# Half of an attention's split products from float32r to float16, from the second batch on

## The chip, the core and the metric

The kernel runs on one core of a Trainium2 chip. The metric is the device time of one execution in microseconds (us); lower is better. The names of the engines are those of the profile: PE (TensorE matmul), PEld (its weight loads), DVE (VectorE), ACT (ScalarE), POOL (GpSimd), SP (SyncE, which issues all DMAs here).

## What is computed

A linear attention with exponential features feeds a feed-forward layer (called MoE in the code; it has one expert). All inputs are float32.

```python
batch, n_heads, seq, head_dim = (8, 8, 576, 64); d_feat = 128
def phi(x):
    proj = np.einsum('bhsd,df->bhsf', x, w_phi)
    proj = proj - np.max(np.abs(proj), axis=-1, keepdims=True)
    return np.concatenate([np.exp(proj), np.exp(-proj)], axis=-1)
q_p, k_p = (phi(q), phi(k))
kv = np.einsum('bhsf,bhsd->bhfd', k_p, v)
z = np.sum(k_p, axis=2)
num = np.einsum('bhsf,bhfd->bhsd', q_p, kv)
den = np.einsum('bhsf,bhf->bhs', q_p, z)[..., None] + 1e-06
x = (num / den), heads side by side: 4608 rows x 512
h = x @ w_in                                  # 512 x 2048
out = (h * (1.0 / (1.0 + np.exp(-1.702 * h)))) @ w_out   # 2048 x 512
```

In the code t is the projection less its largest magnitude. exp(t) is at most 1; exp(-t) can be large.

## The kernel before

The program is first recorded and then put in order by a list scheduler (class Recorder): each operation has an estimated cost, a priority from a table of due times (`R.part(v0, v1)`; one unit is 384 rows through the MoE), and the buffers that it needs. The scheduler simulates the five engines with these costs and emits all instructions in the order that comes out. Every instruction so has the same source line, L346, and each engine works through its list strictly in that order.

**Attention.** A batch has four pairs of heads (hp 0 to 3); a pair is a unit, so there are 32 units, 0 to 31. Units 0 to 5 are "exact" (plain float32 products); the 26 units from 6 on are not, and of these the change speaks most. A unit covers 512 of the 576 positions; the other 64 of all heads are a batch's tail (`attn_tail`). In a unit that is not exact, every factor of a product is split into a high part and a low part, and three of the four partial products are summed in PSUM. For k and for q and for each head (four times a unit), `features_k` or `features_q` makes e = [exp(t), exp(-t)] (128 x 1024, two ACT instructions), and `parts` makes eh = e rounded to float32r (one ACT copy of 1024) and el = e - eh (one DVE subtraction of 1024). v is split in the same way into vs (one ACT copy, one DVE subtraction). The products kv <- vs,eh and vs,el then run: a hi matmul of 132 columns (the weights are eh, the moving operand both parts of v) and a lo matmul of 66 (weights el, moving the high part of v). The first half (s = 0) of e is exp(t), the second (s = 1) exp(-t). The sum kf is split into kzs (ACT copy, then a subtraction, on POOL from batch 1 on), and the numerators and denominators are the products kzs,eh (132) and kzs,el (66). The division makes xf, which is split into float16 halves xo and transposed by DMA into x[b], the MoE's input. The tail's products are vts,ekth/ektl and kzs,eqth/eqtl.

**MoE.** Each factor is split into two float16 parts with power-of-two scales. One step j (16 a chunk) has 12 matmuls hb <- x,wbuf a 384 rows, then ACT th (tanh), DVE g, ACT gh, DVE gl, and 9 matmuls ab <- wbuf,gh/gl of 512 columns. Attention of later batches is interleaved with the chunks. There are three x buffers; x[b] takes the place of x[b-3] (for batch 2: of `kept`, the half sums of the first 512 rows) when the MoE has read it.

**Scales.** `batch_max(sb, stage)` finds the largest magnitude of v for two batches: two DMAs of 1152 KB into the new x buffer, each followed by a DVE reduction of 2304 columns, and then `vg`, its power of two. Before, `csx` = vg * 2^-13 enters only at the division, in `inverse`, and the part has priority u + 0.975 (u is the batch's due time), so the first units of a batch do not wait for it.

Of the kernel before, what the change touches and what calls it, by code (L numbers as in the profile page):

```python
# [20 lines left out]
P = 128  # L21
D = 64
# [327 lines left out]
def attn_moe_kernel(ctx, tc, q, k, v, w_phi, w_in, w_out, out):  # L350
# [25 lines left out]
    def static(name, shape, dt):  # L376
# [13 lines left out]
        e=([P, 1024], F32), eh=([P, 1024], F32R), el=([P, 1024], F32R),  # L390
        ekth=([P, 1024], F32R), ektl=([P, 1024], F32R),
        eqth=([P, 1024], F32R), eqtl=([P, 1024], F32R),
# [9 lines left out]
    }  # L402

# [175 lines left out]
    csx = static("csx", [P, B // SB], F32)  # L579
# [70 lines left out]

    pools["zt"] = buf("zt", [P, 2, NHP, 2, D], F16, 1)
# [7 lines left out]
    nc.gpsimd.memset(f32(vs0), 0.0)  # L659
    nc.gpsimd.memset(f32(vs0[:, :, 0, D : D + 1]), 1.0)  # L660
    nc.gpsimd.memset(f32(vt0), 0.0)
# [3 lines left out]
    for a in range(2):  # L665
        r = slice(a * D, a * D + D)
        nc.gpsimd.memset(f32(vt0[r, :, a, 0, D : D + 1]), 1.0)
# [78 lines left out]
    def features_k(t, exact, hi="eh", lo="el"):  # L746

        e = new("e")
        e4 = e.rearrange("p (a s f) -> p a s f", a=4, s=2)
        R.scalar.activation(e4[:, :, 0], t, AF.Exp)  # L750
        R.scalar.activation(e4[:, :, 1], t, AF.Exp, scale=-1.0)
        return [x.rearrange("p (a f) -> p a f", a=4) for x in parts(e, exact, hi, lo)]

    def features_q(t, exact, hi="eh", lo="el"):
# [6 lines left out]
        R.scalar.activation(e2[:, 0], qt, AF.Exp)  # L761
        R.scalar.activation(e2[:, 1], qt, AF.Exp, scale=-1.0)
        return [x.rearrange("p (s n) -> p s n", s=2) for x in parts(e, exact, hi, lo)]

    def attn_tail(tl, exact, bank):
# [6 lines left out]
        ekt = features_k(tk, False, "ekth", "ektl")  # L772
        eqt = features_q(tq, False, "eqth", "eqtl")
        vt = new("vts")
        for a in range(2):
            r = slice(a * D, a * D + D)
            R.scalar.copy(vt[r, :, a, 0, 0:D], tl[r, 2])
            R.vector.tensor_sub(vt[r, :, a, 1, 0:D], tl[r, 2], f32(vt[r, :, a, 0, 0:D]))
        return ekt, eqt, vt
# [27 lines left out]
    def attn_unit(b, hp, nat, tail, nt, x32, x16, exact, bank):  # L807
# [5 lines left out]
        if exact:  # L813
            tk = project_whole(kq[:, 0], bank)
        else:
            scales = kq_scales(kq)
            tk = project(kq[:, 0], (scales[0], scales[0]), bank)
        if exact:
            vv = vn
        else:  # L820
            vv = new("vs")
            R.scalar.copy(vv[:, :, 0, 0:D], vn[:, :, 0:D])
            R.vector.tensor_sub(vv[:, :, 1, 0:D], vn[:, :, 0:D], f32(vv[:, :, 0, 0:D]))
        kf = new("kf")
        if exact:
            kvt = psa()[0:DV]
            for h in range(2):
                ek = features_k(tk[h], exact)[0]
                mm = [(vv[:, 4 * h + t], ek[:, t]) for t in range(4)]
                for i, k in ((0, 0), (0, 1), (1, 0)):  # L830
                    mm.append((vt[:, hp, h, k], ekt[i][:, hp]))
                products(True, True, [(x, y, kvt[:, 256 * h : 256 * h + 256]) for x, y in mm])
            across(kvt, kf.rearrange("p s h d -> p h s d"))
        for h in range(0 if exact else 2):
            ek = features_k(tk[h], exact)
            kv = psa()[:, 0 : 4 * DV].rearrange("p (s c) -> p s c", s=2)
            mm = []
            for t in range(5):
                for s in range(2):
                    f = slice(s * NF, (s + 1) * NF)  # L840
# [9 lines left out]
        R.scalar.copy(kz[:, :, :, 0], kf)  # L850
        (R.vector if b == 0 else R.gpsimd).tensor_sub(
            kz[:, :, :, 1], kf, f32(kz[:, :, :, 0])
        )
# [10 lines left out]
        def numden(slots, dst):  # L864
# [6 lines left out]
            for i, (h, j) in enumerate(slots):  # L871
                for s in range(2):
                    if j < 4:
                        st = [e[:, s, j * P : (j + 1) * P] for e in eqs[h]]
                        o, m = nd[:, i].unsqueeze(1), kz[:, s, h : h + 1]
                    else:
                        st = [e[:, s, hp * P : (hp + 1) * P] for e in eqt]
                        o, m = nd[:, i : i + 2], kz[:, s]
# [18 lines left out]
        def inverse(den, n):  # L897
# [3 lines left out]
                rc, den, EPS, csx[:, b // SB : b // SB + 1], ALU.add, ALU.mult  # L901
# [27 lines left out]
        if x32 is not None:  # L929
            j0 = TX // P  # L930
            tp = psa()
            for j in range(j0):
                R.tensor.transpose(tp[:, j * P : (j + 1) * P], xj[:, j], ident)
            R.scalar.activation(
                x32[:, hp], tp[:, 0:TX], AF.Copy, scale=csx[:, b // SB : b // SB + 1]
            )
# [160 lines left out]
    xs = {}  # L1097
    V1 = (-1.1375, 0.5)
# [9 lines left out]
    def attention(b):  # L1108
# [105 lines left out]
```

## Time and profile before

| | |
|---|---|
| median of 3 runs | 1141.74 us (1139.68 to 1143.14) |
| the profiled execution, its own time | 1139.36 us |
| its span in the trace | 1137.6 us |
| PE busy | 1098.4 us (97%), 8879 matmuls |
| DVE busy | 846.4 us (74%) |
| ACT busy | 706.1 us (62%) |
| POOL busy | 176.9 us (16%) |
| mean granted TensorE clock | 0.986 |

Busy is the time in which an engine had at least one instruction in work. Matmuls overlap in the pipeline, so a matmul's own duration is not what it costs PE; the distance from its start to the next one's is. The 1.8 us between span and time lie outside the trace.

### The profile page before, as it was taken

The page shows a single profiled execution, that of the slowest core. Times are in us where ns is not written, and L with a number is a line of the kernel's source. Part 1 is how long each engine was busy: PE and PEld are TensorE (multiplying, and loading weights), DVE is VectorE, ACT ScalarE, POOL GpSimd, SP SyncE. Part 2 cuts the span into 40 slices and gives each one's busy share as a digit, 9 for nine tenths or more (in the row PEclk, how much of TensorE's full clock was granted, in tenths as well). Part 3 has the DMA queues.
Part 4 walks back from the last instruction along what each step waited for, and adds up shares of the span by engine and source line. Part 5 has one row for each costly group of instructions (what it writes and reads, how often), then busy time and mean ns, then how long its engine had stood idle before and what let it go on. Part 6 is the DMA issues. An engine that isn't in the chain of part 4 may idle for free.

```text
span 1137.6 us, 22238 instructions
## 1 busy us (share of the span) xinstructions
PE 1098.4 (97%) x8879; PEld 842.6 (74%) x8879; DVE 846.4 (74%) x1642; ACT 706.1 (62%) x1333; POOL 176.9 (16%) x169
## 2 busy tenths in 40 slices
PE   5997999999999999999999999989999999999997
PEld 4664667878887778778888787778887788767653
DVE  5899978999779888786669988887577976523322
ACT  4676786874767766674667766665566776533323
POOL 6545000120111211020011211120111211110000
PEclk9997999999999999989999999989999999999999
DMA  8854214344223262332133243332232230010101
GB/s 270 282 162 148 43 38 95 78 100 124 60 63 80 56 159 57 80 84 48 27 77 79 67 109 96 70 84 48 33 80 57 48 66 11 10 38 1 28 1 28
DMA packets 172520, 87.76 MB, mean 77 GB/s; under 512 B 140032, under 2 KB 164736, under 8 KB 171392
## 3 DMA queue, kind: packets, MB, share of 16 engines
q1 hardware_dynamic: 172416, 86.34, 31.1%
q8 instruction: 69, 1.13, 0.4%
q14 instruction: 35, 0.29, 0.1%
HBM read 54.59 MB, written 9.44 MB: 56 GB/s over the span
## 4 chain that ended last, share of the span: by engine, by line
PE 87%; DVE 6%; ACT 2%; DMA 2%; issue 1%; POOL 1%; SPq 1%; ACTq 0%; DVEq 0%; POOLq 0%
PE ab L346 34%; PE hb L346 32%; PE at L346 21%; DVE el L346 1%; DVE sm L346 1%; DMA x<-in_v_dram 1%; DVE gl L346 1%; DVE sc L346 1%; SPq L346 1%; DVE wbuf L346 1%; DVE t L346 1%; DVE g L346 0%; DMA xT<-xs 0%; ACT e L346 0%; DVE ks L346 0%
## 5 line engine op out<-in xcount | busy, mean ns | idle before, releaser
L346 PE MATMUL hb<-x,wbuf 128*128 128x192 f16 (+3 forms) x3264 | 490.8, 285 | 1.9 <-DVE g L346 1.9
L346 PE MATMUL ab<-wbuf,gh 128*128 128x512 f16 x1152 | 348.2, 386 | 0.8 <-ACT gh L346 0.7
L346 PEld LDWEIGHTS <-wbuf 128*128 128x128 f16 x3264 | 286.3, 99 | 65.8 <-issue 2.8
L346 ACT ACTIVATE th<-hb,usc 128x384 f32<-128x384 f32 (+1 forms) x208 | 115.6, 556 | 143.1 <-PE hb L346 139.5
L346 PE MATMUL ab<-wbuf,gl 128*128 128x512 f16 x576 | 201.2, 386 | 0.5 <-DVE gl L346 0.3
L346 DVE SCALAR_TENSOR_TENSOR g<-th,hb 128x384 f32<-128x384 f32 (+1 forms) x208 | 107.6, 518 | 108.5 <-ACT th L346 106.2
L346 PEld LDWEIGHTS <-gh 128*128 128x128 f16 x1152 | 110.8, 98 | 79.8 <-ACT gh L346 2.4
L346 DVE TENSOR_TENSOR el<-e,eh 128x1024 fp32r<-128x1024 f32 x104 | 128.1, 1233 | 38.9 <-ACT eh L346 20.4
L346 PE MATMUL at<-kzs,eh 128*128 128x132 f32 x416 | 156.2, 378 | 0.1
L346 PE MATMUL at<-vs,eh 128*128 128x132 f32 x416 | 153.6, 372 | 2.6 <-ACT e L346 1.5
L346 PE MATMUL at<-vs,el 128*128 128x66 f32 x416 | 144.2, 347 | 1.2 <-DVE el L346 1.2
L346 PE MATMUL at<-kzs,el 128*128 128x66 f32 x416 | 144.9, 351 | 0.4 <-DVE el L346 0.4
L346 ACT ACTIVATE gh<-g,al 128x384 f16<-128x384 f32 (+1 forms) x176 | 106.5, 606 | 62.1 <-DVE g L346 61.9
L346 DVE SCALAR_TENSOR_TENSOR gl<-g,al,gh 128x384 f16<-128x384 f32 (+1 forms) x176 | 113.0, 642 | 43.1 <-ACT gh L346 36.8
L346 ACT CAST eh<-e 128x1024 fp32r<-128x1024 f32 x104 | 108.8, 1047 | 3.8 <-PE at L346 2.8
L346 DVE TENSOR_REDUCE sm<-at 128x4 f32<-128x512 f32 x126 | 86.1, 684 | 32.3 <-PE at L346 32.1
L346 POOL TENSOR_TENSOR xf<-nf,rc 128x512 f32<-128x512 f32 x28 | 31.1, 1111 | 454.0 <-DVE rc L346 374.6
L346 PE MATMUL at<-ph,xT 128*128 128x128 f16 x944 | 90.7, 221 | 0.0
L346 PEld LDWEIGHTS at<-vs,eh 128*128 128x128 f32 x416 | 84.4, 203 | 6.8 <-ACT e L346 1.7
L346 DVE SCALAR_TENSOR_TENSOR t<-at,ks,sm 128x512 f32<-128x512 f32 x118 | 87.9, 745 | 1.7
L346 PEld LDWEIGHTS at<-kzs,eh 128*128 128x128 f32 x416 | 84.2, 202 | 6.7 <-issue 2.9
L346 PEld LDWEIGHTS <-gl 128*128 128x128 f16 x576 | 56.3, 98 | 43.5 <-DVE gl L346 2.7
(157 smaller groups left out, 1722.5 us busy)
## 6 DMA issues: line engine op xcount, KB each, us to landing
x<-in_v_dram SPq DMA_DIRECT2D x8, 1152.0 KB, 6.1
vn<-in_v_dram SPq DMA_DIRECT2D x64, 128.0 KB, 2.8
kq<-in_k_dram SPq DMA_DIRECT2D x32, 256.0 KB, 3.0
kq<-in_q_dram SPq DMA_DIRECT2D x32, 256.0 KB, 2.9
x<-in_moe_w_in_dram SPq DMA_DIRECT2D x10, 512.0 KB, 5.1
x<-in_moe_w_out_dram SPq DMA_DIRECT2D x10, 512.0 KB, 5.5
out_dram<-osb SPq DMA_DIRECT2D x40, 128.0 KB, 2.4
out_dram<-osb SPq DMA_DIRECT2D x16, 256.0 KB, 2.4
```

Source lines behind the costliest of these rows:

```text
L346: f(*[g(a) for a in o.args], **{k: g(a) for k, a in o.kw.items()})
```

## The change

From batch 1 on, everything that belongs to exp(t) (s = 0) is held in float16: eh6, el6 and their like for the tail, the split of v (v6, vt6) and the split of kf (kz6). What belongs to exp(-t) (s = 1) stays float32r. Both sets of products add into the same PSUM tiles. For the range of float16, v is first multiplied by iv = 1/vg, a power of two; `csx` is then a constant except in batch 0, and its piece at the transposition (dead code here, TX = 0) goes. In detail:

- `parts` has no copy any more: ACT computes exp twice, once into e (float32) and once straight into the high part, each 512 wide; DVE subtracts 512 at a time. The float32r pools shrink to 512.
- `split_v`: ACT writes the float16 high part of v * iv, DVE the float32r low part, and POOL copies each into the other type.
- kz is split per s: two ACT copies and two POOL subtractions of 132 in place of one of 264.
- `batch_max` is put earlier in the due times (u - 0.1 in place of u + 0.975), and the v split of batches 2, 4 and 6 needs its result.
- Exact units: the tail's three products of 256 columns a head become six of 128.

```diff
-        e=([P, 1024], F32), eh=([P, 1024], F32R), el=([P, 1024], F32R),
+        e=([P, 1024], F32), eh=([P, 512], F32R), el=([P, 512], F32R),
...
+    for nm in ("eh", "el", "ekth", "ektl", "eqth", "eqtl"):
+        pools[nm + "6"] = buf(nm + "6", [P, 512], F16, NB[nm])
...
+        R.vector.reciprocal(iv[:, sb : sb + 1], vg[:, sb : sb + 1])
...
-    def parts(e, exact, hi, lo):
+    def two(nm, b, spare):
+
+        return new(nm + "6") if b else new(spare), new(nm)
+
+    def parts(b, src, e, hi, lo):
+
+        his, los = two(hi, b, "eh"), two(lo, b, "el")
+        for i, sg in enumerate((1.0, -1.0)):
+            R.scalar.activation(e[i], src, AF.Exp, scale=sg)
+            R.scalar.activation(his[i], src, AF.Exp, scale=sg)
+            h = his[i] if i == 0 and b else f32(his[i])
+            R.vector.tensor_sub(los[i], e[i], h)
+        return list(zip(his, los))
...
-        eh, el = new(hi), new(lo)
-        R.scalar.copy(eh, e)
-        R.vector.tensor_sub(el, e, f32(eh))
-        return eh, el
...
+    def split_v(dst, d16, src, sc):
+
+        R.scalar.activation(d16[0], src, AF.Copy, scale=sc)
+        R.vector.scalar_tensor_tensor(dst[1], src, sc, d16[0], ALU.mult, ALU.subtract)
+        R.gpsimd.tensor_copy(dst[0], d16[0])
+        R.gpsimd.tensor_copy(d16[1], f32(dst[1]))
...
-            R.scalar.copy(vv[:, :, 0, 0:D], vn[:, :, 0:D])
-            R.vector.tensor_sub(vv[:, :, 1, 0:D], vn[:, :, 0:D], f32(vv[:, :, 0, 0:D]))
+            vv = (new("v6"), new("vs"))
+            split_v(
...
-                    st = [e[:, t, f] for e in ek] if t < 4 else [e[:, hp, f] for e in ekt]
-                    vx = vv[:, 4 * h + t] if t < 4 else vt[:, hp, h]
+                    st = [e[:, t] for e in ek[s]] if t < 4 else [e[:, hp] for e in ekt[s]]
+                    vx = vv[s][:, 4 * h + t] if t < 4 else vt[s][:, hp, h]
...
+            kz = [new("kz6"), kz[:, 1]]
+            for s in range(2):
+                R.scalar.copy(kz[s][:, :, 0], kf[:, s])
+                R.gpsimd.tensor_sub(
+                    kz[s][:, :, 1], kf[:, s], f32(kz[s][:, :, 0]) if s else kz[s][:, :, 0]
+                )
...
-                R.part(u + 0.975, u + 0.975)
+                z = u - VB if b else u + 0.975
+                R.part(z, z)
```

The scheduler makes a new order of it. On PE, in the middle of the kernel, while the MoE reads the third x buffer (x_114), the rows before read as follows (hb and ab are the MoE; kzs and vs with eh or el are float32r products, whose weight load is part of the instruction; a float16 product has a row LDWEIGHTS of its own):

```order
L346 LDWEIGHTS wbuf_156
L346 MATMUL hb_65<-x_114,wbuf_156 128x384
L346 MATMUL at_62<-kzs_105,eh_97 128x132
L346 LDWEIGHTS wbuf_156
L346 MATMUL hb_65<-x_114,wbuf_156 128x384
L346 MATMUL at_62<-kzs_105,el_98 128x66
L346 LDWEIGHTS wbuf_156
L346 MATMUL hb_65<-x_114,wbuf_156 128x384
L346 MATMUL at_62<-kzs_105,eh_97 128x132
```

Now, at the like place (v and its eh, el here are the float16 ones):

```order
L346 MATMUL at_63<-vs_180,eh_97 128x132
L346 LDWEIGHTS gh_120
L346 MATMUL ab_67<-wbuf_165,gh_120 128x512
L346 MATMUL at_63<-vs_180,el_98 128x66
L346 LDWEIGHTS eh_141
L346 MATMUL at_63<-v_183,eh_141 128x132
L346 LDWEIGHTS gl_122
L346 MATMUL ab_67<-wbuf_165,gl_122 128x512
L346 MATMUL at_61<-kzs_105,eh_96 128x132
L346 LDWEIGHTS el_144
L346 MATMUL at_63<-v_183,el_144 128x66
```

A float32r product still has a MoE matmul ahead of it; every second attention product is now a float16 one, which may stand behind a float32r one.

On DVE, where batch 2 begins, the v split of unit 8 stood before ahead of both reductions of batch_max (sc <- x), at 0.92 units of MoE progress, with the maximum's power of two (vg) far behind, after unit 10's split. The rows there now (g and gl are the MoE's):

```order
L346 TENSOR_REDUCE sc_138<-sc_137 128x1
L346 SCALAR_TENSOR_TENSOR gl_121<-g_117,al_172,gh_119 128x256
L346 TENSOR_REDUCE sc_133<-at_62 1x1
L346 SCALAR_TENSOR_TENSOR gl_122<-g_118,al_172,gh_120 128x256
L346 TENSOR_SCALAR sc_133<-sc_133 1x1 x2
L346 COPY vg_179<-at_62 128x1
L346 TENSOR_SCALAR osc_177<-mg_173,vg_179 128x1
L346 TENSOR_SCALAR usc_176<-wg_169,vg_179 128x1 x2
L346 RECIPROCAL iv_175<-vg_179 128x1
L346 SCALAR_TENSOR_TENSOR vs_180<-vn_71,iv_175,v_183 128x8x64
L346 SCALAR_TENSOR_TENSOR vts_181<-tl_88,iv_175,vt_184 64x4x64 x2
```

The first v split of batch 2 stands right behind iv, at 1.67 units of MoE progress in place of 0.92; by unit 11 (2.19 in both) the two orders are level again, and from unit 17 on the new one is level or up to half a unit ahead (unit 25: 7.12 before, 6.94 now).

On POOL a unit in the middle of the kernel read kzs, xf, xo before; now:

```order
L346 CAST vs_180<-v_183 128x8x64
L346 CAST v_183<-vs_180 128x8x64
L346 TENSOR_TENSOR kz_182<-kf_106,kz_182 128x2x66
L346 TENSOR_TENSOR kzs_105<-kf_106,kzs_105 128x2x66
L346 TENSOR_TENSOR xf_104<-nf_109,rc_139 128x2x4x64
L346 TENSOR_TENSOR xo_111<-xf_104,xo_111 128x512
```

Two copies have come in ahead of the subtractions, and one subtraction has become two of half the size.

## Rows read from the trace of the kernel before

**Rows 1.** Windows by stretch: busy us (instructions) by engine, clock, DMA share, GB/s.

```profile
0.00:140.00 140.00, 116.39 (x677) 78.79 (x678) 118.81 (x226) 89.42 (x172) 65.40 (x59) 0.95 0.60 184
140.00:481.80 341.80, 340.85 (x2981) 270.26 (x2978) 293.11 (x591) 236.46 (x465) 40.99 (x40) 1.00 0.35 81
481.80:509.40 27.60, 25.11 (x220) 21.81 (x219) 22.69 (x55) 19.05 (x35) 7.18 (x7) 0.88 0.41 100
744.00:771.80 27.80, 24.62 (x218) 21.04 (x217) 23.61 (x52) 21.31 (x39) 7.08 (x6) 0.88 0.33 86
771.80:1000.30 228.50, 228.50 (x1931) 183.55 (x1929) 162.35 (x301) 143.64 (x269) 31.04 (x32) 1.00 0.22 44
```

**Rows 2.** Groups by form, PE: count, busy us, mean ns, idle before them.

```profile
L346 PE MATMUL at<-kzs,eh 128*128 128x132 f32 x416 | 156.2, 378 | 0.1
L346 PE MATMUL at<-vs,eh 128*128 128x132 f32 x416 | 153.6, 372 | 2.6 <-ACT e L346 1.5 <-ACT eh L346 0.7 <-ACT ls L346 0.3
...
L346 PE MATMUL at<-ph,xT 128*128 128x128 f16 x944 | 90.7, 221 | 0.0
...
L346 PE MATMUL at<-vts,ekth 128*128 128x132 f32 x104 | 39.3, 379 | 0.0
...
L346 PE MATMUL at<-kzs,eqth 128*128 128x264 f32 x52 | 22.0, 440 | 0.0
...
L346 PE MATMUL hb<-x,wbuf 128*128 128x64 f16 x192 | 10.7, 194 | 0.0
```

**Rows 3.** Timeline of PE, 369 to 371 us: start, duration, instruction, count.

```profile
368.97 1.46 PE L346 MATMUL hb<-x,wbuf 128*128 128x384 f16 x8
...
370.30 0.34 PE L346 MATMUL hb<-x,wbuf 128*128 128x384 f16 x1
370.34 0.36 PE L346 MATMUL at<-vs,eh 128*128 128x132 f32 x1
370.54 0.34 PE L346 MATMUL hb<-x,wbuf 128*128 128x384 f16 x1
370.58 0.33 PE L346 MATMUL at<-vs,el 128*128 128x66 f32 x1
370.75 0.34 PE L346 MATMUL hb<-x,wbuf 128*128 128x384 f16 x1
```

**Rows 4.** Timeline of PE: float16 matmuls of 128 and of 64 columns.

```profile
278.77 0.41 PE L346 MATMUL hb<-x,wbuf 128*128 128x64 f16 x8
...
366.05 0.61 PE L346 MATMUL at<-ph,xT 128*128 128x128 f16 x8
```

**Rows 5.** Groups by form, DVE and ACT: the split before and its nearest kin.

```profile
L346 DVE TENSOR_TENSOR el<-e,eh 128x1024 fp32r<-128x1024 f32 x104 | 128.1, 1233 | 38.9 <-ACT eh L346 20.4 <-PE at L346 18.2
...
L346 ACT CAST eh<-e 128x1024 fp32r<-128x1024 f32 x104 | 108.8, 1047 | 3.8 <-PE at L346 2.8
...
L346 ACT ACTIVATE e<-t 128x512 f32<-128x512 f32 x144 | 86.5, 629 | 2.2 <-DVE el L346 1.7 <-PE at L346 0.4
...
L346 DVE TENSOR_TENSOR vs<-vn,vs 128x512 fp32r<-128x512 f32 x26 | 17.9, 688 | 8.7 <-ACT vs L346 8.5
```

**Rows 6.** Groups by form, POOL: a subtraction and a copy.

```profile
L346 POOL TENSOR_TENSOR kzs<-kf,kzs 128x264 fp32r<-128x264 f32 x28 | 21.2, 756 | 278.4 <-ACT kzs L346 266.7 <-issue 11.7
...
L346 POOL COPY wb<-wst 64x128 f32<-64x128 f32 x2 | 0.6, 304 | 1.4 <-DMA wst<-in_w_phi_dram 1.3
```

**Rows 7.** Timeline of all engines, 889 to 892 us: POOL and DVE at the same time.

```profile
889.43 1.88 POOL L346 TENSOR_TENSOR xo<-xf,xo 128x512 f16<-128x512 f32 x1 [1.73 <-ACT xo L346]
890.21 1.52 DVE L346 SCALAR_TENSOR_TENSOR gl<-g,al,gh 128x384 f16<-128x384 f32 x1
```

**Rows 8.** Timelines of DVE and PE: unit 20's v split and its first product.

```profile
606.64 0.69 DVE L346 TENSOR_TENSOR vs<-vn,vs 128x512 fp32r<-128x512 f32 x1
...
624.84 0.33 PE L346 MATMUL at<-vs,eh 128*128 128x132 f32 x1
```

**Rows 9.** DMA issues, and the group of batch_max's reductions on DVE.

```profile
x<-in_v_dram SPq DMA_DIRECT2D x8, 1152.0 KB, 6.1
...
L346 DVE TENSOR_REDUCE sc<-x 128x1 f32<-128x2304 f32 x8 | 20.3, 2543 | 0.9 <-DMA x<-in_v_dram 0.9
```

More of the change, by code (lines that the diff above doesn't have):

```diff
@@ L649, in attn_moe_kernel @@
     pools["vts"] = buf("vts", [P, NHP, 2, 2, DV], F32R, 1)
+    pools["kz6"] = buf("kz6", [P, 2, 2, DV], F16, 1)
+    pools["v6"] = buf("v6", [P, 8, 2, DV], F16, 1)
+    pools["vt6"] = buf("vt6", [P, NHP, 2, 2, DV], F16, 1)
     pools["zt"] = buf("zt", [P, 2, NHP, 2, D], F16, 1)
@@ L658, in attn_moe_kernel @@
     vs0, vt0 = pools["vs"].aps[0], pools["vts"].aps[0]
-    nc.gpsimd.memset(f32(vs0), 0.0)
-    nc.gpsimd.memset(f32(vs0[:, :, 0, D : D + 1]), 1.0)
-    nc.gpsimd.memset(f32(vt0), 0.0)
+    v60, vt60 = pools["v6"].aps[0], pools["vt6"].aps[0]
+    for ap in (f32(vs0), v60, f32(vt0), vt60):
+        nc.gpsimd.memset(ap, 0.0)
+    for ap in (f32(vs0), v60):
+        nc.gpsimd.memset(ap[:, :, 0, D : D + 1], 1.0)
     nc.gpsimd.memset(pools["zt"].aps[0], 0.0)
@@ L666, in attn_moe_kernel @@
         r = slice(a * D, a * D + D)
-        nc.gpsimd.memset(f32(vt0[r, :, a, 0, D : D + 1]), 1.0)
+        for ap in (f32(vt0), vt60):
+            nc.gpsimd.memset(ap[r, :, a, 0, D : D + 1], 1.0)
     def kq_scales(kq):
@@ L771, in attn_tail @@
             tk, tq = project(n, kq_scales(tl[:, 0:2]), bank)
-        ekt = features_k(tk, False, "ekth", "ektl")
-        eqt = features_q(tq, False, "eqth", "eqtl")
+        ekt = features_k(b, tk, False, "ekth", "ektl")
+        eqt = features_q(b, tq, False, "eqth", "eqtl")
         vt = new("vts")
+        if b == 0:
+            for a in range(2):
+                r = slice(a * D, a * D + D)
+                R.scalar.copy(vt[r, :, a, 0, 0:D], tl[r, 2])
+                R.vector.tensor_sub(
+                    vt[r, :, a, 1, 0:D], tl[r, 2], f32(vt[r, :, a, 0, 0:D])
+                )
+            return ekt, eqt, (vt, vt)
+        vt6 = new("vt6")
         for a in range(2):
             r = slice(a * D, a * D + D)
-            R.scalar.copy(vt[r, :, a, 0, 0:D], tl[r, 2])
-            R.vector.tensor_sub(vt[r, :, a, 1, 0:D], tl[r, 2], f32(vt[r, :, a, 0, 0:D]))
-        return ekt, eqt, vt
+            split_v(
+                [vt[r, :, a, i, 0:D] for i in range(2)],
+                [vt6[r, :, a, i, 0:D] for i in range(2)],
+                tl[r, 2],
+                iv[r, b // SB : b // SB + 1],
+            )
+        return ekt, eqt, (vt6, vt)
     def products(first, last, mm):
@@ L817, in attn_unit @@
             tk = project(kq[:, 0], (scales[0], scales[0]), bank)
+        sc = iv[:, b // SB : b // SB + 1]
         if exact:
-            vv = vn
-        else:
-            vv = new("vs")
-            R.scalar.copy(vv[:, :, 0, 0:D], vn[:, :, 0:D])
-            R.vector.tensor_sub(vv[:, :, 1, 0:D], vn[:, :, 0:D], f32(vv[:, :, 0, 0:D]))
+            if b:
+                R.scalar.activation(vn[:, :, 0:D], vn[:, :, 0:D], AF.Copy, scale=sc)
+        else:
+            vv = (new("v6"), new("vs"))
+            split_v(
+                [vv[1][:, :, i, 0:D] for i in range(2)],
+                [vv[0][:, :, i, 0:D] for i in range(2)],
+                vn[:, :, 0:D],
+                sc,
+            )
         kf = new("kf")
@@ L827, in attn_unit @@
             for h in range(2):
[L828 to L832, printed above, removed]
+                ek = features_k(b, tk[h], True)
+                o = kvt[:, 256 * h : 256 * h + 256]
+                mm = [(vn[:, 4 * h + t], ek[:, t], o) for t in range(4)]
+                for s in range(2):
+                    for i, k in ((0, 0), (0, 1), (1, 0)):
+                        mm.append(
+                            (vt[s][:, hp, h, k], ekt[s][i][:, hp], o[:, s * NF : s * NF + NF])
+                        )
+                products(True, True, mm)
             across(kvt, kf.rearrange("p s h d -> p h s d"))
         for h in range(0 if exact else 2):
-            ek = features_k(tk[h], exact)
+            ek = features_k(b, tk[h], False)
             kv = psa()[:, 0 : 4 * DV].rearrange("p (s c) -> p s c", s=2)
@@ L849, in attn_unit @@
         kz = new("kzs")
[L850 to L853, printed above, removed]
+        if b == 0:
+            R.scalar.copy(kz[:, :, :, 0], kf)
+            R.vector.tensor_sub(kz[:, :, :, 1], kf, f32(kz[:, :, :, 0]))
+            kz = [kz[:, s] for s in range(2)]
+        else:
+            kz = [new("kz6"), kz[:, 1]]
+            for s in range(2):
+                R.scalar.copy(kz[s][:, :, 0], kf[:, s])
+                R.gpsimd.tensor_sub(
+                    kz[s][:, :, 1], kf[:, s], f32(kz[s][:, :, 0]) if s else kz[s][:, :, 0]
+                )
         if exact:
@@ L900, in inverse @@
             R.vector.tensor_scalar(
-                rc, den, EPS, csx[:, b // SB : b // SB + 1], ALU.add, ALU.mult
+                rc, den, EPS, csx if b == 0 else 2.0**-13, ALU.add, ALU.mult
             )
@@ L910, in attn_unit @@
                 products(
-                    True, True, [(kf[:, s, h], eqs[h][0][:, s], ndt) for s in range(2)]
+                    True, True, [(kf[:, s, h], eqs[h][:, s], ndt) for s in range(2)]
                 )
@@ L928, in attn_unit @@
         xj = xf.rearrange("p j a d -> p j (a d)")
[L929 to L936, printed above, removed]
         if exact:
```

54 lines of the change are left out of this document (29 added, 25 removed).

## The prediction

> **What bounds the kernel now.** I read the windows by stretch first [rows 1]. From 140 us on PE is the bound: it is busy for 340.85 of 341.80 us up to 481.8 us, and for all of 771.8 to 1000.3 us. DVE is the next engine, with 293.11 of 341.80 us (86%) in the first of these stretches and 71% in the second; ACT has 69% and 63%. Three places differ. In the first 140 us PE idles for 23.6 us while the weights arrive and DVE is busy for 118.81 us. At 481.8 to 509.4 us and at 744.0 to 771.8 us PE loses 2.5 and 3.2 us idle, and the granted clock is 0.88, so part of each stretch ran at 1.2 GHz in place of 2.4: some 3.3 us more in each (0.12 of 27.7). There the MoE has used up the x that it has, and attention is what PE waits for. Everything else is PE's own work, so a saving on PE counts nearly whole, if the others keep up.
>
> Then the groups of PE [rows 2] give the counts, and the timelines [rows 3, 4] what a matmul really costs. The reader is to look at starts, not durations. Eight MoE matmuls of 384 columns take 1.46 us with the last one's 0.34 in it: 0.16 us each. From 370.30 to 370.75 there are two of these and one float32r pair (132 and 66 columns): 0.45 - 0.32 = 0.13 us for the pair, though each of them shows over 0.33 us. Eight float16 matmuls of 128 columns take 0.61 us with a last one of 0.22 [rows 2, 4], so 56 ns each; of 64 columns (0.41 - 0.19) / 7 = 31 ns, each with a weight load of its own.
>
> **The change, step by step.** The sum is made against the profiled execution's 1139.4 us, which is 2.4 us under the median of the runs shown.
>
> *Products in float16.* Of 416 + 416 + 104 pairs [rows 2] half become float16: 468. By columns a float16 pair costs 58 + 32 = 90 ns, against 130: 40 ns saved, give or take 10 for the rounding of the rows. 468 x 0.04 = **-18.7 us** (-14 to -23.4). A row speaks for this price at every spacing: float16 weights of 128 columns are reloaded every 31 ns there. The Trainium skill would give less: "TensorE: Matmul & The Clock Gate", section "Back-to-back issue gap", puts a stream of weight loads and matmuls at about 81 ns a matmul for 128 columns in a real kernel. By that a float16 hi product is no cheaper than it is now in float32r, and the sum would be near -8 us. The trace's 56 ns for just that form disagrees, and goes first.
>
> *Tail of the queries.* 26 of 52 products of 264 columns and their lo partners [rows 2], at the saving of a pair: **-1.0 us**.
>
> *Exact units.* 36 products of 256 columns become 72 of 128: the columns stay, and 36 starts come on top, at 0 to 0.08 us each (a float32r pair's 0.13 less its columns is 0.05 for two). **+1 us** (0 to +3), the most of it in the first 200 us, where PE has idle time.
>
> *Splits on ACT and DVE.* DVE: 2 x 688 in place of 1233 ns [rows 5], 143 ns more for each of 120 splits (104 and 16 of the tails): 17 us. ACT: four exponentials of 629 ns in place of two and a copy of 1047: 211 ns more, 25 us, and some 8 us for the scaled copies of v and the two halves of kz. Consecutive instructions overlap, so these are upper ends. What hides them is PE's work: DVE has 49 us free in 140 to 481.8 us, where ten of the 26 units lie and at most 7 of the 17 us fall. **0**; without that cover, up to +17. The chain itself gets shorter: the high part no longer waits for e and a copy.
>
> *v split and POOL.* A POOL copy of 512 columns is not in the trace; it lies between one of 128 columns, 304 ns [rows 6], and four times that, 1.2 us. Two of them add 0.6 to 2.4 us behind the DVE step. At unit 20 the product needs vs 17.5 us after the split ended (607.33 to 624.84) [rows 8]. **0.** If that cover were gone it would be 26 x 2.4 = 62 us, but the split's place in the order is as early as before in all batches but 2.
>
> *kz in halves.* One subtraction of 756 ns [rows 6] becomes two: 0.38 each if the time goes with the columns, 0.76 each if it doesn't. The products of s = 0 need only the first. A copy of v may stand ahead in POOL's queue. 0 to +0.4 us a unit, so 0 to +10; I take **0**, since between exp(t)'s half and the other's PE has float16 work.
>
> *batch_max earlier.* Two DMAs of 6.1 us and two reductions of 2.5 us [rows 9] make a chain of 17 us, and behind it on DVE stand g and gl of the MoE. Before, DVE waited 0.9 us for it in all. Now the v split of batches 2, 4 and 6 waits for iv. At batches 4 and 6 the split stands where it stood (progress 3.69 and 3.69, 6.69 and 6.62), at batch 2 0.75 units later. A DMA half late at each place would be 3 x 3 us; **+1 us** (0 to +9).
>
> *The two stalls.* By the order unit 25 comes at 6.94 units of progress in place of 7.12, so attention is a little ahead at the second stall; unit 17 (4.12) is not. Both stalls together cost 12 us (above). **-2 us** (0 to -12).
>
> Sum: -18.7 - 1.0 + 1 + 1 - 2 = -19.7 us, so 1119.7 us on the profiled execution and **1122 us** as a median.
>
> **Rivals.**
>
> *Batch 2 starts too late (slower or no change).* Place: 1.67 to 2.56 units of progress, where units 8 to 11 are now done. A unit of MoE is 16 steps of 12 matmuls of 384 columns at 0.16 us [rows 3] and 9 of 512 at the same rate: 61 us. In 140 to 481.8 us lie ten units of attention (6 to 15) and, by the order's progress at the first and the last of them, some 3.6 of MoE, so a unit of attention is (342 - 220) / 10 = 12 us of PE. For DVE, with about 1.2 us of g and gl a step (an estimate from gl and g at the rate of vs [rows 5], 0.55 us each), it is (293 - 65) / 10 = 23 us. Between 1.67 and 2.56 DVE has 4 x 23 + 0.89 x 18 = 108 us and PE 4 x 12 + 0.89 x 61 = 102: nearly level, so a loss of 6 us. If what needs no v isn't done ahead and all four units press into the half unit from 1.67 to 2.19, PE has 80 us against DVE's 101 and loses 21. It decides from 20 us on: 1141 us on the profiled execution, 1143 as a median. Against it: exp(k) and the projections need no iv and can go ahead of it, and the next units are level with before. Chance 0.11 for slower, 0.07 for a draw, both together with the next rival's worst.
>
> *POOL's copies slow DVE.* At 889 us a POOL subtraction of 1.88 us and a DVE instruction of 1.52 us lie over each other [rows 7]; with 384 columns the latter would be some 0.6 us at the rate of vs [rows 5]. There are 80 copies and 28 more subtractions; at 0.9 us each, if one in three meets such a DVE instruction, DVE gets 32 us, 12 of them in 140 to 481.8 us, where it has 42 left: hidden. PE would see only part, say 5 to 10 us: 1127 to 1132 us as a median. The Trainium skill ("Advanced Engine Details and Errata", section "Mode Summary") has GpSimd share VectorE's second port; these rows agree. Chance 0.12.
>
> *The hi products gain nothing.* If a float16 matmul next to a float32r one costs what the latter does (no row shows the two side by side), only the lo ones gain: the two halves of the pair in [rows 3] take 0.24 - 0.16 = 0.08 and 0.21 - 0.16 = 0.05 us, so 468 x (0.050 - 0.032) = 8 us, and 1134 us as a median. For it only that float32r and float16 stand side by side now; against it, the float16 MoE matmuls in [rows 3], which cost no more beside a float32r one than alone once the pair has its 0.13 us. Chance 0.06.
>
> *More than forecast.* Both stalls go: 10 us more, 1112 us. Chance 0.12.
>
> **How the numbers follow.** The forecast itself, 1114 to 1127 us, has 0.52. With 0.12 for more, 0.12 and 0.06 for the two rivals that leave a part of the gain, faster by over 0.3% has 0.82, a draw within 0.3% (3.4 us, about what runs from 1139.7 to 1143.1 can tell) 0.07, slower 0.11. The range is 1109 to 1137 us: below, the two stalls gone and the upper end of the pair's saving; above, the draw and the slower case and part of the third rival stay outside, 0.19 in all with the little below 1109.
>
> **What would show it.** PE's busy time should fall by about 19 us, with 0.09 us from start to start for a float16 pair. DVE should rise by 5 to 17 us and ACT by 15 to 33, with PE idle no longer than now in 140 to 481.8 us (1 us). The stretch from 140 to 481.8 us should be the shorter by its share of pairs, 7 us. Idle time of PE before the first products of unit 8, behind DVE's iv, would show the first rival; DVE differences of 512 columns well over 0.69 us beside POOL copies the second; float16 pairs 0.13 us apart the third. The forecast is wrong if DVE is over 95% busy anywhere between 285 and 480 us.

## The result, and the profile after

The changed kernel takes 1124.35 us (median of 4 runs, 1121.42 to 1127.12), the kernel before 1140.71 us (1139.43 to 1143.14): a ratio of 0.985, 95% interval 0.982 to 0.989. The forecast was 1122 us, with 1109 to 1137 as its range. The profiled execution has a span of 1121.8 us, 15.8 less than before. Executions of one kernel differ by some us with the granted clock: the changed kernel took 1121.42 us at a mean of 0.992 and 1127.12 at 0.988. The sum held; two of its terms did not, and partly cancelled.

Two lines of the page of the changed kernel: each engine's busy us, share of the span and instructions, and the group of the MoE's first matmuls (busy us, mean ns of one, idle time ahead of them and what ended it).

```profile
PE 1078.0 (96%) x8915; PEld 775.0 (69%) x8915; DVE 862.5 (77%) x1763; ACT 713.7 (64%) x1483; POOL 228.2 (20%) x282
...
L346 PE MATMUL hb<-x,wbuf 128*128 128x192 f16 (+3 forms) x3264 | 479.8, 281 | 6.2 <-DVE g L346 5.9
```

The same group in the kernel before:

```profile
L346 PE MATMUL hb<-x,wbuf 128*128 128x192 f16 (+3 forms) x3264 | 490.8, 285 | 1.9 <-DVE g L346 1.9
```

PE works 20.4 us less and idles 4.6 us more (span less busy: 43.8 against 39.2). Where, is seen in the windows by stretch, at the same cuts as [rows 1]:

```profile
0.00:140.00 140.00, 117.55 (x703) 79.54 (x704) 118.48 (x231) 90.13 (x176) 65.73 (x68) 0.96 0.59 184
140.00:481.80 341.80, 334.12 (x2994) 246.32 (x2993) 301.54 (x641) 240.29 (x525) 66.20 (x88) 1.00 0.35 81
481.80:509.40 27.60, 25.35 (x242) 20.89 (x239) 24.42 (x52) 20.34 (x42) 6.73 (x8) 0.94 0.38 103
744.00:771.80 27.80, 27.80 (x283) 23.46 (x281) 22.55 (x50) 19.72 (x41) 3.54 (x6) 1.00 0.33 86
771.80:1000.30 228.50, 226.79 (x1921) 164.22 (x1919) 161.78 (x323) 142.60 (x299) 37.34 (x52) 1.00 0.22 46
```

Against [rows 1], the second row has PE idle for 7.68 us where it was 0.95. The fourth has no idle time and full clock, where 3.18 us were idle and the clock was 0.88: the second stall is gone. The first stall is only half better (clock 0.94, still 2.25 us idle). In the second row PE works 6.73 us less and idles 6.73 us more: the stretch that was to be 7 us shorter got no shorter. By the MoE matmuls that lie ahead of 481.8 us, both kernels have done 4.0 units there, with about as much of attention, so all of the gain comes behind that point.

The price of a pair stands in PE's timeline of the changed kernel: start, duration, instruction. vs with eh and el is the float32r pair, v with eh and el the float16 one.

```profile
640.18 0.33 PE L346 MATMUL hb<-x,wbuf 128*128 128x384 f16 x1
640.21 0.36 PE L346 MATMUL at<-vs,eh 128*128 128x132 f32 x1
640.40 0.34 PE L346 MATMUL hb<-x,wbuf 128*128 128x384 f16 x1
640.45 0.33 PE L346 MATMUL at<-vs,el 128*128 128x66 f32 x1
640.61 0.24 PE L346 MATMUL at<-v,eh 128*128 128x132 f16 x1
640.69 0.19 PE L346 MATMUL at<-v,el 128*128 128x66 f16 x1
640.72 0.33 PE L346 MATMUL hb<-x,wbuf 128*128 128x384 f16 x1
```

From 640.18 to 640.72 PE gets through two MoE matmuls (0.16 each), one float32r pair and one float16 pair. That leaves 0.22 us for both pairs. Over the whole trace the median spacings give 124 ns for the float32r pair and 88 for the float16 one: 36 ns less, and 468 x 36 = 16.8 us. (The 88 are 58 + 30 with a MoE matmul behind each. In the rows above it is 73 + 29 to the next starts, but the float32r product that follows then starts 30 ns behind its MoE matmul in place of 44, so the sum is the same.)

What is new on the other side, in the groups by form of DVE and POOL (columns as for the group above):

```profile
L346 DVE TENSOR_TENSOR el<-e,eh 128x512 f16<-128x512 f32 x104 | 73.6, 708 | 13.9 <-PE at L346 7.3 <-ACT eh L346 6.4
...
L346 DVE SCALAR_TENSOR_TENSOR vs<-vn,iv,v 128x512 fp32r<-128x512 f32 x26 | 24.1, 926 | 4.5 <-ACT v L346 4.2
...
L346 DVE TENSOR_REDUCE sc<-x 128x1 f32<-128x2304 f32 x8 | 20.4, 2548 | 4.2 <-DMA x<-in_v_dram 4.2
...
L346 POOL CAST vs<-v 128x512 fp32r<-128x512 f16 x26 | 19.7, 757 | 130.7 <-ACT v L346 77.0 <-issue 46.7 <-PE at L346 6.8
```

PE's wait ahead of the MoE's first matmuls, 5.9 us of it for DVE's g, is in the group above; before it was 1.9. DVE's wait for batch_max's loads went from 0.9 us [rows 9] to 4.2. And vs, 688 ns as a plain subtraction [rows 5], takes 926.

Where the largest wait for g comes from is seen in the timelines of DVE and PE: the reduction of batch_max waits for its load, and g stands behind it.

```profile
260.61 2.55 DVE L346 TENSOR_REDUCE sc<-x 128x1 f32<-128x2304 f32 x1 [1.82 <-DMA x<-in_v_dram]
263.08 0.74 DVE L346 SCALAR_TENSOR_TENSOR g<-th,hb 128x256 f32<-128x256 f32 x2
...
263.55 0.68 PE L346 MATMUL hb<-x,wbuf 128*128 128x64 f16 x14 [1.85 <-DVE g L346]
```

Two more of these waits (1.59 us at 407 and 0.73 us at 418 us) also end with a g that stands behind such a reduction: 4.2 us in all.

### The profile page after: what moved, and what is told of

It is laid out like the page before. It is cut to its first block, busy times and chain, and to the rows that moved or that the text cites. A ratio compares the mean times of both kernels' runs of the same rounds, so it can differ in the third digit from the quotient of the medians.

```text
span 1121.8 us, 22818 instructions
## 1 busy us (share of the span) xinstructions
PE 1078.0 (96%) x8915; PEld 775.0 (69%) x8915; DVE 862.5 (77%) x1763; ACT 713.7 (64%) x1483; POOL 228.2 (20%) x282
## 4 chain that ended last, share of the span: by engine, by line
PE 77%; DVE 12%; ACT 5%; DMA 3%; issue 2%; SPq 1%; POOL 0%; ACTq 0%; DVEq 0%; POOLq 0%
PE ab L346 30%; PE hb L346 28%; PE at L346 19%; DMA xT<-xs 2%; DVE el L346 2%; DVE sm L346 2%; DVE t L346 1%; ACT e L346 1%; DVE gl L346 1%; DVE g L346 1%; DVE ks L346 1%; ACT eh L346 1%; DVE sc L346 1%; DVE vs L346 1%; DVE xs L346 1%
## 5 line engine op out<-in xcount | busy, mean ns | idle before, releaser
L346 PE MATMUL hb<-x,wbuf 128*128 128x192 f16 (+3 forms) x3264 | 479.8, 281 | 6.2 <-DVE g L346 5.9
L346 DVE TENSOR_TENSOR el<-e,eh 128x512 f16<-128x512 f32 (+1 forms) x210 | 145.9, 708 | 18.8 <-PE at L346 9.3
L346 PE MATMUL at<-ph,xT 128*128 128x128 f16 x944 | 98.7, 222 | 0.3
L346 ACT ACTIVATE e<-at 128x512 f32<-128x512 f32 x144 | 85.7, 604 | 20.7 <-PE at L346 19.3
L346 ACT ACTIVATE e<-t 128x512 f32<-128x512 f32 x144 | 89.4, 637 | 5.5 <-DVE t L346 3.7
L346 PE MATMUL at<-kzs,eh 128*128 128x132 f32 x216 | 79.8, 376 | 0.0
L346 PE MATMUL at<-vs,eh 128*128 128x132 f32 x208 | 79.5, 382 | 0.0
L346 PEld LDWEIGHTS <-xT 128*128 128x128 f16 x944 | 67.1, 99 | 13.9 <-issue 0.5
L346 PE MATMUL at<-kzs,el 128*128 128x66 f32 (+1 forms) x212 | 73.3, 351 | 0.0
L346 PE MATMUL at<-vs,el 128*128 128x66 f32 x208 | 73.3, 352 | 0.0
```

What stands on the lines that cost most here:

```text
L346: f(*[g(a) for a in o.args], **{k: g(a) for k, a in o.kw.items()})
```

## The experiments

Each is timed against the kernel before on the same chip; ratios are to that, with 95% intervals.

**Float32r again, planned at float16's cost.** The planner is told that these products cost what float16 ones do; the order is made anew, and is alike in kind.

```diff
-        pools[nm + "6"] = buf(nm + "6", [P, 512], F16, NB[nm])
+        pools[nm + "6"] = buf(nm + "6", [P, 512], F32R, NB[nm])
...
-            vv = (new("v6"), new("vs"))
+            vv = [new("vs")] * 2
...
-            wide = mybir.dt.size(ap[1].dtype) == 4
+            wide = mybir.dt.size(ap[1].dtype) == 4 and ap[1].tensor.name.split("_")[0][:-1] not in SIX
```

> The changed kernel with everything of exp(t) held in float32r again: two exponentials, splits 512 wide, scaled v, kz in halves and the early batch_max stay; POOL's copies of v go, since both halves can read one v. The planner's costs of the matmuls are held at those of float16. Theory (the float16 pair is what pays, 124 against 88 ns in the changed kernel's trace, 468 x 36 ns = 17 us, and the rest is worth nothing or costs a little): PE busy back at 1095 to 1100 us, 1139 to 1146 us. Rival (a good part of the gain comes from the shorter split chain): under 1133 us, with PE busy near 1098 but its idle time well under 39 us.

1159.11 us, ratio 1.016 (1.014 to 1.017), PE busy for 1126.6 us: worse than either theory. PE's timeline of this run shows why:

```profile
607.30 0.34 PE L349 MATMUL hb<-x,wbuf 128*128 128x384 f16 x1
607.35 0.36 PE L349 MATMUL at<-kzs,eh 128*128 128x132 f32 x1
607.55 0.34 PE L349 MATMUL hb<-x,wbuf 128*128 128x384 f16 x1
607.59 0.33 PE L349 MATMUL at<-kzs,el 128*128 128x66 f32 x1
607.75 0.31 PE L349 MATMUL at<-kzs,eh 128*128 128x132 f32 x1
607.90 0.24 PE L349 MATMUL at<-kzs,el 128*128 128x66 f32 x1
607.98 0.34 PE L349 MATMUL hb<-x,wbuf 128*128 128x384 f16 x1
```

It is the pattern of 640.18 above, with float32r in the place of the float16 pair: 0.68 us in place of 0.54. Less the two MoE matmuls, 0.355 us are left for two pairs; with 0.124 for the one whose halves stand apart, the other costs 0.23. So a float32r pair has two prices, 0.124 us with a MoE matmul ahead of each half and 0.23 us right behind another float32r product. The planner, told that these products are as light as float16, put 337 of them in the dear place (counted over the trace): 337 x 0.14 = 47 us, next to the 48.6 us that PE is busier than in the changed kernel. (The other 131 pairs at 36 ns would add 5 us, and the first stall, at full clock in this run, takes 1.7 off.)

**Float32r again, with the planner's own costs.** As the last, without its third edit.

> The all-float32r kernel of e1_all_f32r once more, but with the planner's own costs for float32r, so that it spreads these matmuls between those of the MoE as it does in the kernel before. Theory (a float32r product costs 124 ns a pair when MoE matmuls lie between and 223 ns back to back, so e1 paid for its order; float16 itself is worth 36 ns a pair): PE busy at 1093 to 1098 us as in e4_before_early, 1132 to 1139 us. Rival (the split's new form costs on its own): over 1142 us.

1141.15 us, ratio 1.001 (1.000 to 1.001): no change from before, and 2 us above the range expected. PE is busy for 1103.0 us, since the first stall grew, as its window shows:

```profile
481.80:509.40 27.60, 25.02 (x169) 22.11 (x167) 21.35 (x48) 19.85 (x45) 7.96 (x10) 0.69 0.30 76
```

At 0.69 of the clock 0.31 x 27.6 = 8.6 us of this window are lost, against 1.7 in the changed kernel. Of the 25.0 us of PE's busy time between the two kernels that leaves some 18 for float16 itself, by the pair's price 16.8. The restructured split, the scaled v and the early batch_max together bring nothing without float16, in the order that came of them; POOL's copies of v are not needed in this run.

**The other half in float16 too.** The changed kernel's order is kept.

```diff
-        kzs=([P, 2, 2, 2, D + 2], F32R)
+        kzs=([P, 2, 2, 2, D + 2], F16)
...
-        for i, sg in enumerate((1.0, -1.0)):
+        for i, sg in enumerate((1.0, 1.0)):
```

> The changed kernel in its own order, with the other half of the products in float16 too; exp(-t) is replaced by exp(t) so that nothing overflows, so the numbers are not those of the reference. Theory (PE is the bound nearly everywhere, and a pair costs 36 ns less): 468 x 36 ns = 17 us less, 1105 to 1110 us, PE busy at 1059 to 1063 us. Rival (DVE has become the bound beside it): 1114 us or more, with PE's idle time up by over 8 us.

1115.50 us, ratio 0.977 (0.976 to 0.978): 8.9 us less than the changed kernel, where PE's price promised 17. The engines' line of its page:

```profile
PE 1064.7 (96%) x8915; PEld 706.5 (63%) x8915; DVE 863.1 (77%) x1763; ACT 713.4 (64%) x1483; POOL 229.6 (21%) x282
```

PE works only 13.3 us less, and its idle time is up by 5.3, to 49.1 us (1113.8 - 1064.7). The time is the rival's; the idle time grew by 5.3 us and not by the 8 that it asked for. So half of the second saving is lost, most of it to waits. The other 3.5 us stand in PE's busy time, though its pairs have the promised spacing (57 and 29 ns, or 61 and 29 right behind each other); some 1.4 us are the clock of the first 140 us (0.95 against 0.96), the rest stays open. It ran with all engines in the order made for the dearer products, so it is no bound for a plan of its own.

**batch_max moved alone, in the kernel before.**

```diff
-                R.part(u + 0.975, u + 0.975)
+                z = u - 0.1 if b else u + 0.975
+                R.part(z, z)
```

> The kernel before with batch_max alone moved, from u + 0.975 to u - 0.1. Nothing but the division needs its result there. Theory (DVE stands at the two reductions until the loads land, and g and gl stand behind it): 2 to 4 us more, 1143 to 1145 us, with DVE's waits for the loads up from 0.9 to about 4 us. Rival (what costs is the v split that waits for iv, not the place of the reductions): 1139.5 to 1142 us.

> The kernel before with batch_max at u + 0.8 in place of u + 0.975, nothing else. Theory (the stalls at 482 and 744 us come of divisions that stand behind a late vg; 0.175 units earlier is 11 us earlier, enough for most of it): 1133 to 1137 us, granted clock at the second stall 0.94 or more. Rival (it takes the place ahead of the batch, and in e2_const it is the float16 that removes the stall): 1139.5 to 1142 us.

Both theories fell in both runs. At u - 0.1 the kernel before takes 1133.66 us, ratio 0.994 (0.992 to 0.995), 7.0 us less. At u + 0.8, between the two places, it takes 1155.68 us, ratio 1.013 (1.011 to 1.015), 14.6 us more. The windows at the two stalls, of u - 0.1:

```profile
481.80:509.40 27.60, 25.73 (x237) 22.07 (x237) 25.58 (x55) 20.14 (x37) 6.44 (x7) 0.94 0.43 112
...
744.00:771.80 27.80, 27.72 (x261) 23.07 (x259) 22.69 (x48) 21.72 (x40) 4.53 (x6) 1.00 0.35 86
```

and of u + 0.8:

```profile
481.80:509.40 27.60, 22.29 (x190) 20.30 (x188) 24.70 (x55) 18.70 (x33) 6.03 (x6) 0.81 0.45 113
...
744.00:771.80 27.80, 24.02 (x181) 18.77 (x179) 23.16 (x42) 18.25 (x32) 5.34 (x4) 0.84 0.37 90
771.80:1000.30 228.50, 227.39 (x1948) 186.92 (x1948) 165.89 (x317) 145.31 (x272) 26.96 (x28) 0.98 0.24 47
```

At u - 0.1 the second stall is gone (3.1 us of idle time and 3.3 us of clock), and the first is half better (0.6 and 1.7): 8.7 us, of which 7.0 reach the time. These are the clocks of the changed kernel at both stalls, 0.94 and 1.00, without any float16 product. At u + 0.8 both stalls are worse, and the second reaches into the next stretch, where the clock is 0.98 (4.6 us). A place 11 us (0.175 units of 61 us) earlier on paper makes a new order of what stands behind it: 4440 of the 8879 places in PE's list hold another matmul than before, 3190 at u - 0.1. That the order sets how far attention has come when the MoE has used up its x is the likely reading; no run moves batch_max in the kernel before with the rest of the order held.

**No wait for 1/vg.** v scaled by the constant 1, vg in the division again, batch_max at two later places.

```diff
+    R.gpsimd.memset(iv, 1.0)
...
-        R.vector.reciprocal(iv[:, sb : sb + 1], vg[:, sb : sb + 1])
...
-                z = u - VB if b else u + 0.975
+                z = u + (0.8 if b else 0.975)
```

> The changed kernel with v scaled by the constant 1 in place of 1/vg (vg comes in at the division again) and batch_max due at u + 0.8 in place of u - 0.1. Theory (the new idle time of PE at 252 to 280, 392 to 421 and 671 us, some 6 us, is DVE standing at the reductions behind the 1152 KB loads and the v split behind iv): 1117 to 1120 us, idle time before hb <- x,wbuf back at about 2 us. Rival (DVE simply has too much to do in that place, so that a wait taken away comes back as another): 1122 to 1126 us.

> e2_const with batch_max at u + 0.45 in place of u + 0.8. Theory (with no v split behind vg the place matters little as long as the divisions don't wait): 1120 to 1123 us. Rival (an earlier place still helps the batch's first divisions): under 1119 us.

1121.47 us at u + 0.8 (ratio 0.983, 0.982 to 0.984), 1125.08 us at u + 0.45 (0.987, 0.985 to 0.989). The wait before hb <- x,wbuf falls to 1.2 us in the first, by 5.0, but the time by only 2.9: most of it comes back in small waits elsewhere (idle time 41.8 us in all, against 43.8). Both runs miss both of their expectations, the first by lying between them. The second stall is gone in both, and the first keeps its full clock; at u + 0.8:

```profile
481.80:509.40 27.60, 26.15 (x269) 21.66 (x268) 25.66 (x59) 20.73 (x43) 6.03 (x8) 1.00 0.29 82
```

Against the changed kernel's row that is 0.8 us of idle time and 1.7 of clock, about as much as the 2.9 us gained; how much of the gain the wait is worth, these two runs with orders of their own can't tell.

**The same wait, in an unchanged order.** Three of the four pairs of reductions read a constant, put in place of the loaded tile when the order is written out.

```diff
+            if sb:
+                R.ops[-1].swap = cst.broadcast_to([P, stage.t.shape[1]])
```

> The changed kernel with every engine's order as it is; the reductions of batch_max for batches 2, 4 and 6 read a constant of the same power of two in place of the loaded v. The loads still run, but nobody waits for them, so iv is there as soon as DVE comes to it. Theory (DVE's waits for the loads, 4.2 us, end in PE's idle time before hb <- x,wbuf): 1119 to 1122 us, that idle time down from 6.2 to 2 to 3 us. Rival (DVE has too much to do there, and the idle time comes all the same): 1123 to 1126 us.

1122.83 us, ratio 0.984 (0.983 to 0.985), 1.5 us less than the changed kernel and within the width of the intervals. Its page:

```profile
L350 PE MATMUL hb<-x,wbuf 128*128 128x192 f16 (+3 forms) x3264 | 480.9, 281 | 2.9 <-DVE g L350 2.6
```

The wait falls as the theory said (6.2 to 2.9), but the time doesn't follow by 3.3 us: PE's idle time in 140 to 481.8 us falls only from 7.68 to 6.19. Part of it comes back as a wait for ACT (1.2 us ahead of ab, at 265 us), and the reductions themselves, 2.5 us each, still stand in front of g. In the profiled execution the first stall is deeper too (clock 0.88, 1.7 us):

```profile
140.00:481.80 341.80, 335.61 (x3005) 247.34 (x3004) 303.17 (x643) 241.13 (x528) 66.44 (x88) 1.00 0.36 81
481.80:509.40 27.60, 25.58 (x232) 21.33 (x230) 23.48 (x50) 19.38 (x40) 6.62 (x8) 0.88 0.37 101
```

So the loads are worth 1 to 2 us here, not 5.

**POOL's copies: doubled, and moved to ACT.** Doubled, the order of all else unchanged:

```diff
+            if o.eng == "gpsimd" and o.meth == "tensor_copy" and o.args[0].t.shape == (P, 8, D):
+                self.nc.gpsimd.tensor_copy(self.spare, g(o.args[1]))
```

> The changed kernel with every engine's order as it is, but each of POOL's copies of 512 columns is made a second time, into a spare tile that nobody reads: 52 copies more, some 31 us of POOL. Theory (DVE slows where POOL works, and PE waits for part of it): DVE busy up by 5 to 12 us, 1127 to 1132 us. Rival (hidden behind PE): 1122.5 to 1126 us.

1131.26 us, ratio 0.991 (0.989 to 0.993): 6.9 us more, as the theory had it; DVE is busy for 870.9 us, 8.4 more (POOL's own queue grows too, by 38.8 us of work). Moved to ACT, once as below with a plan of its own, once by naming ACT only when the old order is written out:

```diff
-        R.gpsimd.tensor_copy(dst[0], d16[0])
-        R.gpsimd.tensor_copy(d16[1], f32(dst[1]))
+        R.scalar.copy(dst[0], d16[0])
+        R.scalar.copy(d16[1], f32(dst[1]))
```

> The changed kernel with the two copies of split_v on ACT in place of POOL. Theory (POOL's copies slow DVE where both are at work, and that is part of PE's new idle time): DVE's mean for gl and el falls, PE's idle time falls by 1 to 4 us, 1120 to 1123.5 us. Rival (the slower DVE is hidden behind PE, or 52 copies more make ACT late): 1124 to 1129 us.

> The changed kernel in its own planned order, as in e10_casts_twice, but every copy of split_v runs on ACT at its place in the common order in place of POOL; PE's and DVE's order are untouched. Theory (POOL's copies slow DVE, which e10 showed upwards; e5 also made a new order): vs near 0.75 us in place of 0.93, DVE busy down by 8 to 12 us, 1117 to 1121 us. Rival (e5 gained by its order, and here ACT comes late with what stands behind the copies): 1123 to 1128 us.

With its own plan 1118.35 us, ratio 0.981 (0.979 to 0.983), the lowest median of a kernel here that leaves nothing out, though the interval still touches the changed kernel's. Its trace is of the slowest of the four executions (1123.18 us; the others took 1116.70 to 1119.74). In the old order 1132.61 us, ratio 0.993 (0.992 to 0.994), slower than the changed kernel by 8.3. The v split on DVE with the copies doubled on POOL:

```profile
L346 DVE SCALAR_TENSOR_TENSOR vs<-vn,iv,v 128x512 fp32r<-128x512 f32 x26 | 26.3, 1013 | 4.6 <-ACT v L346 4.2
```

with the copies on ACT, by a plan of its own:

```profile
L346 DVE SCALAR_TENSOR_TENSOR vs<-vn,iv,v 128x512 fp32r<-128x512 f32 x26 | 19.4, 745 | 5.8 <-ACT v L346 5.7
```

and with the copies on ACT in the old order, beside two groups of PE:

```profile
L348 DVE SCALAR_TENSOR_TENSOR vs<-vn,iv,v 128x512 fp32r<-128x512 f32 x26 | 20.1, 775 | 4.4 <-ACT v L348 4.1
...
L348 PE MATMUL ab<-wbuf,gh 128*128 128x512 f16 x1152 | 345.0, 381 | 4.6 <-ACT gh L348 4.4
...
L348 PE MATMUL at<-kz,eh 128*128 128x132 f16 x208 | 47.2, 231 | 5.0 <-ACT eh L348 3.9 <-ACT e L348 0.9
```

Single instructions of the changed kernel show what the means hide, here two v splits on DVE with the copy that POOL starts just behind each:

```profile
642.70 1.19 DVE L346 SCALAR_TENSOR_TENSOR vs<-vn,iv,v 128x512 fp32r<-128x512 f32 x1 [1.44 <-ACT v L346]
642.73 0.61 POOL L346 CAST vs<-v 128x512 fp32r<-128x512 f16 x1 [2.09 <-ACT v L346]
...
868.50 0.74 DVE L346 SCALAR_TENSOR_TENSOR vs<-vn,iv,v 128x512 fp32r<-128x512 f32 x1
868.57 1.14 POOL L346 CAST vs<-v 128x512 fp32r<-128x512 f16 x1
```

One of the two takes its 0.74 or 0.61 us, the other some 0.45 to 0.53 more. With a copy 0.03 us behind it DVE is the one that is held up (six of 26 splits, all 1183 to 1186 ns); with the copy 0.07 us behind it POOL is. Of the 26 splits 13 take 736 to 752 ns. With the copies on ACT by a plan of its own all 26 take 734 to 754.

On average that is 745 ns (775 in the old order) without a copy on POOL beside it, 926 with one copy, 1013 with two: POOL does slow DVE, and DVE's busy time follows (851.9 and 853.4 us without the copies, 862.5, 870.9). The Trainium skill ("Advanced Engine Details and Errata", section "Mode Summary") has GpSimd and VectorE share a port; these rows agree, for an instruction with two tensors to read. The mean of gl (384 columns), which the first expectation wanted lower, hardly moves: 650 ns in the changed kernel, 646 and 639 with the copies on ACT, 654 with them doubled. And DVE's 9 us less in the old order do not decide alone: in the old order PE waits for ACT ahead of these two groups for 4.6 and 5.0 us, in the changed kernel for 0.2 and 2.0 us. How much of the 6.0 us between the medians, with a plan of its own, is the port, how much the new order and how much the spread of the executions stays open.

**Both together.** Constant scale, batch_max at u + 0.8, copies on ACT.

> e2_const and e5_casts_act in one kernel: v scaled by the constant 1, batch_max at u + 0.8, both copies of split_v on ACT. Theory (two separate causes of idle time, 2.9 and 6.0 us less than the changed kernel): 1114 to 1117 us. Rival (they take away the same idle time, or the new order brings a stall back): 1118 to 1122 us.

1120.47 us, ratio 0.981 (0.980 to 0.983): the rival. The two gains, neither of them clear of the spread by itself, do not add; the clock is at 0.94 again at the first stall.

## Why the prediction was right, and where it was not

- *Products in float16*, -18.7: right in mechanism and nearly in size. 124 and 88 ns a pair in place of 130 and 90, so -16.8 us. The rival that hi products gain nothing asked for 18 ns a pair; the 36 measured are twice that, so it fell, although the hi product right behind a float32r one takes 73 ns to the next start (0.08 in the rows above): the rest comes back at the next float32r product. (By its own terms the rival's time was nearer 1133 than 1134 us.) With it fell the sum of near -8 us by the 81 ns that the Trainium skill names for 128 columns ("TensorE: Matmul & The Clock Gate", section "Back-to-back issue gap"); the trace's spacing for that form is still 56 ns. Without the clock's part at the stalls (5.0 us, below) PE's busy time fell by 15.4 us, where the step with the tail and the exact units has -18.7; up to 1.4 of the 15.4 may be the clock of the first 140 us (0.96 against 0.95).
- *Tail* and *exact units*, -1.0 and +1: too small to be seen apart.
- *The two stalls*, -2 (0 to -12): mis-sized. The second went whole (3.2 us idle, 0.12 x 27.8 = 3.3 of clock), of the first 0.2 idle and 0.06 x 27.6 = 1.7 of clock: -8.4 us. The step took the order's progress at two units for the measure. The place of batch_max, which the prediction priced only as a wait, gives the kernel before the same gain at the stalls by itself (8.7 us); with float32r throughout and the early place the second stall goes as well, but the first grows (0.69 of the clock). The two runs of batch_max alone show that a place in the plan moves the time from -7 to +15 us, so it should have been a wide term of its own with both signs. That these 6.4 us more and the waits of the next step partly cancel is luck.
- *Splits on ACT and DVE*, 0, with PE idle from 140 to 481.8 us no longer than before (1 us): this step failed. PE idles for 7.7 us there, and 2.8 us more in the later stretches. DVE's 16.1 us more lay inside the 5 to 17 forecast, but the free 49 us on DVE were not where they were needed: 5.3 of the 7.7 us are waits for g, and 4.2 of these stand right behind a reduction of batch_max (at 263, 407 and 418 us). From 392 to 420 us DVE is 97% busy and PE loses 2.3 of 28 us. The text's own test (over 95% anywhere between 285 and 480) was met, and the forecast held; but the test says little, since the kernel before had met it already, and the changed kernel has a stretch still fuller, both with hardly any idle time on PE (the first row is of the kernel before, the others of the changed one; columns as in [rows 1]):

```profile
352.00:380.00 28.00, 27.93 (x227) 21.04 (x224) 27.45 (x56) 21.73 (x40) 7.54 (x7) 1.00 0.40 93
...
374.00:402.00 28.00, 27.97 (x238) 19.92 (x236) 27.86 (x63) 20.09 (x45) 7.99 (x10) 1.00 0.43 94
392.00:420.00 28.00, 25.69 (x197) 16.72 (x195) 27.04 (x51) 19.39 (x39) 4.29 (x6) 1.00 0.64 180
```

So what costs is not a full DVE, but one that comes late with g. ACT rose by 7.6 us, not 15 to 33: the sum of its durations rose by 38 (790.8 to 829.0), but they overlap.

- *v split and POOL*, 0: the copies take 0.76 and 0.73 us, inside 0.3 to 1.2, and hold up no product at length. Their cost is the one that the rival *POOL's copies slow DVE* named, and a second set of them costs 6.9 us. Of the 7.7 us little is shown to be theirs: in the old order with the copies on ACT, PE's waits for DVE in that stretch fall from 7.0 to 5.4 us, and those for g only from 5.3 to 4.9.
- *batch_max earlier*, +1 (0 to +9): the loads' wait is worth 1.5 us of time in the unchanged order, near the size, though DVE stands there for 4.2 us. But PE's waits behind the reductions, 4.2 us and another 1.2 for sc at 674 us, belong to this step, within its range and far over its middle. What the step left out is that the same edit makes another order, with the stalls above.
- *Batch 2 starts too late*: it didn't come at that size. From 252 to 280 us PE is busy for 24.8 of 28 us (3.2 idle), behind g and the reductions; that is the rival's place at a sixth of its price.

The measured sum: -15.4 for matmuls, -8.4 for the stalls, +6.7 and +2.8 for new waits, some -1.5 at both ends of the kernel: -15.8 us. It is 4 us short of the forecast's -19.7, and made of other parts.

## What to carry to other kernels

On an engine that is 97% busy a cheaper instruction takes its price off that engine's work (some 16 us here), but waits for the next engine take part of it back (9.5 us in the stretches outside the stalls), and of a second saving of the same size only half was left (8.9 us): an engine that is 77% busy has free time only on average. A busy share near 100% in some stretch doesn't tell that it will be waited for; what stands ahead of the awaited instruction does. Where a list scheduler makes the order, any edit, even of one due time, brings a term of its own; here it lay between -7 and +15 us, as much as the edit itself: price it with both signs, and test an edit in an unchanged order beside its own. The planner's cost of an instruction decides where it stands, and what it really costs there can differ by a factor of two.

## What the runs showed of the hardware

A float32r pair of 132 and 66 columns costs 0.124 us with float16 matmuls of 384 or 512 columns between, and 0.23 us right behind another float32r product; a float16 pair costs 0.088 us in that same place (medians of the spacings). A copy of 512 columns on POOL with a change of type takes 0.61 us undisturbed, 0.73 to 0.76 on average. Where it meets a DVE instruction of 512 columns with two tensors to read (0.74 us undisturbed), one of the two can be held up by about half a microsecond while the other isn't: 1.19 and 0.61 us at 642.7, 0.74 and 1.14 at 868.5.
